# Folding a feature map into two projection weights with 32-row TensorE tiles, in two whole-matrix stretches

## The chip, the cores and the metric

The kernel runs on one core of a Trainium2 chip. The metric is the device time of one execution in microseconds (us), lower is better. A profile's span leaves out about 1.7 us of it. TensorE is called PE, its weight loads PEld, VectorE DVE, ScalarE ACT, GpSimd POOL, SyncE SP. PSUM, where matmuls write, has eight banks of 512 fp32 values in each of 128 partitions (the Trainium skill, "PSUM — Partial Sum Buffer", Specifications; the kernel's pools fit it).

## The reference, cut to what matters

```python
qkv = (x @ wqkv)...                      # x: 2048 x 512, bf16; 32 heads of 16
pq = jnp.einsum('bhsd,hdf->bhsf', q, w_phi)     # a 16x16 map per head
pk = jnp.einsum('bhsd,hdf->bhsf', k, w_phi)
phi_q = concat([softmax(pq), softmax(-pq)])     # phi_k likewise; linear attention follows
...
z = gelu(x @ w_in)                       # second branch: 2048 x 1376
z1, z2 = z[..., :688], layernorm(z[..., 688:])
g = w_sp @ z2 + b_sp                     # mixes along the sequence
return gate * attention(...) @ wo + (1 - gate) * (z1 * g) @ w_out
```

As `q @ w_phi` is `x @ (wq @ w_phi)`, the kernel multiplies `w_phi` into `wq` and `wk` once, on the chip, and then projects `x` with the folded weights. That fold is what changes.

Of the kernel before, what the change touches and what calls it, by code (L numbers as in the profile page):

```python
# [14 lines left out]
P = 128  # L15
# [8 lines left out]
NDT = D // P  # L24
CH = 512
# [10 lines left out]
def kernel(  # L36
# [14 lines left out]
    nc = tc.nc  # L51
# [14 lines left out]
    wq_p = pers.tile([P, NDT, D], BF16, name="wq_p")  # L66
    wk_p = kvw.tile([P, NDT, D], BF16, name="wk_p")
# [3 lines left out]
    wqkT = early.tile([P, 8, D], BF16, name="wqkT")  # L71
    wphiE = early.tile([P, H, DH], BF16, name="wphiE")
    eexp = early.tile([P, P], BF16, name="eexp")
    wphi = early.tile([P, NDT, P], BF16, name="wphi")
# [32 lines left out]
        out=ramp[:, 0, :], data0=ones32[:, :], data1=zeros[:, :], initial=0.0,  # L107
# [4 lines left out]
    for q in range(4):  # L112
        qs = slice(32 * q, 32 * q + 32)
        nc.vector.tensor_tensor(
            out=ident[qs, qs], in0=ramp[qs, 0, :], in1=ramp[qs, 1, :], op=ALU.is_equal)
# [3 lines left out]
    def load_z2w(eng, dt):  # L119
# [10 lines left out]
        out=xs[:, 2:4, :], in_=x2[2 * P:4 * P, :].rearrange("(i p) d -> p i d", p=P))  # L130
    for h in range(2):
        nc.sync.dma_start(
            out=w_z1[:, 2 * h:2 * h + 2, :], in_=w_in_v[:, 2 * h:2 * h + 2, 0:FH])
    for i in range(4, 8):
        nc.sync.dma_start_transpose(out=xT[:, :, i * P:(i + 1) * P], in_=x2[i * P:(i + 1) * P, :])
    for q in range(2, NCH):
        nc.sync.dma_start_transpose(
            out=xT[:, :, q * CH:(q + 1) * CH], in_=x2[q * CH:(q + 1) * CH, :]
# [4 lines left out]
        out=wv_sb[:, :, :],  # L143
        in_=A_wqkv[:, 2 * D:3 * D].rearrange("(dt p) n -> p dt n", p=P),
    )
    for q in range(NCH):
        nc.sync.dma_start_transpose(
            out=wspT[:, :, q * CH:(q + 1) * CH], in_=B_w_sp[q * CH:(q + 1) * CH, :]
# [4 lines left out]
        out=eexp[:, :], in_=eexp[:, :], pattern=[[0, 8], [-1, 16]],  # L153
# [4 lines left out]
        out=mask_bd[:], in_=mask_bd[:], pattern=[[-16, 8], [0, 16]],  # L158
# [3 lines left out]
        out=mask_bd[:], in_=mask_bd[:], pattern=[[16, 8], [0, 16]],  # L162
# [4 lines left out]
        out=mask4[:], in_=mask4[:], pattern=[[-32, NG]],  # L167
# [3 lines left out]
        out=mask4[:], in_=mask4[:], pattern=[[32, NG]],  # L171
# [3 lines left out]
        out=mask64[:, :, :], in_=mask4[:, :, None].to_broadcast([P, NG, DH]))  # L175
# [7 lines left out]
    def next_turn(kind, n):  # L183
        turn[kind] += 1
        return f"{kind}{(turn[kind] - 1) % n}"

    def zp_tile():
        return psA.tile([P, 2, CH], FP32, name="zp", tag=next_turn("zp", 3))

    def pq_tile(shape, dtype=FP32):  # L190
        return psF.tile(shape, dtype, name="pq", tag=next_turn("pq", 2))
# [24 lines left out]
    def z2_tile(tt):  # L216
        z2_out(tt, z_mm(tt, w_z2, FH + 1))

    def z2_first_two():
        zps = [zp_tile() for _ in range(2)]  # L220
        tp1 = psA.tile([P, 2, P], BF16, name="tp1", tag=next_turn("zp", 3))
        turn["zp"] -= 1

        def warm_up(n, w=CH):
            for _ in range(n):
                nc.tensor.matmul(  # L226
                    zps[0][:, 1, 0:w], lhsT=nc.const_aps.tensor(1.0, [P, P], BF16),
                    rhs=nc.const_aps.tensor(1.0, [P, w], BF16), start=True, stop=True)

        def one(tt, dt, j):  # L230
            z_one(zps[tt], tt, w_z2, FH + 1, dt, j)

        warm_up(6)
        warm_up(5, P)
        x_T(0, 0, 1, pq_tile([P, 1, P], BF16)[:, :, :])
        x_T(0, 1, NDT, pq_tile([P, 3, P], BF16)[:, :, :], on_act=True)
        warm_up(3, P)
        one(0, 0, 0)
        x_T(1, 0, 2, tp1[:, :, :])
        x_T(1, 2, NDT, pq_tile([P, 2, P], BF16)[:, :, :], on_act=True)  # L240
        one(0, 1, 0)
        warm_up(2, P)
        one(1, 0, 0)
        one(1, 1, 0)
        gate_T()
        one(0, 2, 0)
        one(1, 2, 0)
        for dt in range(2):
            one(0, dt, 1)
            one(1, dt, 1)  # L250
        one(0, 2, 1)
        one(1, 2, 1)
        x_T(2, 0, NDT, pq_tile([P, NDT, P], BF16)[:, :, :])
        one(0, 3, 0)
        one(0, 3, 1)
        z2_out(0, zps[0])
        one(1, 3, 0)
        one(1, 3, 1)
        z2_out(1, zps[1])
        x_T(3, 0, NDT, pq_tile([P, NDT, P], BF16)[:, :, :])  # L260

    def z1_tile(tt):
        zp = z_mm(tt, w_z1, FH)
        nc.scalar.activation(  # L264
            out=z1all[:, tt, :].rearrange("p (j n) -> p j n", j=2), in_=zp[:, :, 0:HF],
            func=AF.Gelu_apprx_tanh,
        )

    def z2_norm(ts):
        sl = slice(ts[0], ts[-1] + 1)  # L270
        nc.gpsimd.tensor_scalar(
            out=veps[:, sl], in0=mv[:, sl, 1], scalar1=1e-5, scalar2=None, op0=ALU.add
        )
        nc.gpsimd.tensor_tensor(out=rstd[:, sl], in0=veps[:, sl], in1=mhalf[:, sl], op=ALU.pow)
        for tt in ts:
            nc.vector.tensor_scalar(
                out=z2all[:, tt, :], in0=z2all[:, tt, :],
                scalar1=mv[:, tt, 0:1], scalar2=rstd[:, tt:tt + 1],
                op0=ALU.subtract, op1=ALU.mult,
            )  # L280
# [16 lines left out]
    def b_T():  # L297
        bt = pq_tile([P, NT])
        nc.tensor.matmul(bt[:, :], lhsT=brow[:, :], rhs=ident[:, 0:NT], start=True, stop=True)
        nc.vector.tensor_copy(out=bT[:, :], in_=bt[:, :])  # L300

    def wphi_fold():
        wps = pq_tile([P, NDT, P])
        for kc in range(NDT):
            nc.tensor.matmul(  # L305
                wps[:, kc, :], lhsT=eexp[:, :],
                rhs=wphiE[:, kc * 8:(kc + 1) * 8, :].rearrange("e h f -> e (h f)"),
                start=True, stop=True,
            )
        nc.vector.tensor_tensor(  # L310
            out=wphi[:, :, :], in0=wps[:, :, :],
            in1=mask_bd[:, None, :].to_broadcast([P, NDT, P]), op=ALU.mult,
        )

    def fold(qk, dt):
        dst = wq_p if qk == 0 else wk_p
        fps = pq_tile([P, CH])
        for kc in range(NDT):
            nc.tensor.matmul(  # L319
                fps[:, kc * P:(kc + 1) * P],  # L320
                lhsT=wqkT[:, qk * 4 + kc, dt * P:(dt + 1) * P],
                rhs=wphi[:, kc, :],
                start=True, stop=True,
            )
        if dt % 2 == 1:
            nc.scalar.copy(out=dst[:, dt, :], in_=fps[:, :])
        else:
            nc.vector.tensor_copy(out=dst[:, dt, :], in_=fps[:, :])

    with tc.manual_schedule(engines={mybir.EngineType.PE, mybir.EngineType.Activation}):  # L330
        z2_first_two()
        z2_tile(2)
        z2_tile(3)
        b_T()
        for c in range(NCH):
            ts = list(range(c * 4, c * 4 + 4))
            for tt in ts:
                if c > 0:
                    z2_tile(tt)
                if c >= 2 and tt % 2 == 0:  # L340
                    fold(3 - c, (tt % 4) // 2)
            for tt in ts:
                z1_tile(tt)
                if c >= 2 and tt % 2 == 0:
                    fold(3 - c, 2 + (tt % 4) // 2)
            z2_norm(ts)
            if c == 1:
                wphi_fold()
# [264 lines left out]
```

## The kernel before: the parts that the change touches

The first stage makes 32 z tiles (16 for z2, 16 for z1) from 8 matmuls each, in four groups c = 0..3 of four z2 and four z1 tiles. A z tile takes two PSUM banks, and three such buffers (`zp0` to `zp2`) rotate. Two single banks (`pq0`, `pq1`) serve everything else of the stage. That is all eight banks. PE and ACT run in program order. DVE's order is chosen by the scheduler at build time.

```python
def zp_tile():
    return psA.tile([P, 2, CH], FP32, name="zp", tag=next_turn("zp", 3))

def pq_tile(shape, dtype=FP32):
    return psF.tile(shape, dtype, name="pq", tag=next_turn("pq", 2))

def z2_out(tt, zp):                      # gives the buffer zp back
    z2v = z2all[:, tt, :].rearrange("p (j n) -> p j n", j=2)
    nc.scalar.activation(out=z2v, in_=zp[:, :, 0:HF], func=AF.Gelu_apprx_tanh)
    nc.vector.tensor_copy(out=glog[:, tt:tt + 1], in_=zp[:, 1, HF:HF + 1])   # "the glog copy"
    for j in range(2):
        nc.vector.bn_stats(out=bn6[:, tt, j, :], in_=z2v[:, j, :])
    nc.vector.bn_aggr(...)
# z1_tile: 8 matmuls into a zp, then one gelu on ACT gives it back
# z2_norm(ts): POOL makes rstd, then DVE normalises the group's four z2 tiles

def fold(qk, dt):                        # 128 rows of a folded weight
    dst = wq_p if qk == 0 else wk_p
    fps = pq_tile([P, CH])
    for kc in range(NDT):
        nc.tensor.matmul(
            fps[:, kc * P:(kc + 1) * P],
            lhsT=wqkT[:, qk * 4 + kc, dt * P:(dt + 1) * P],
            rhs=wphi[:, kc, :],          # 128x128, eight 16x16 blocks on the diagonal
            start=True, stop=True,
        )
    # copied out by DVE (even dt) or ACT (odd dt)
...
    for c in range(NCH):
        ...
        for tt in ts:
            if c > 0: z2_tile(tt)
            if c >= 2 and tt % 2 == 0: fold(3 - c, (tt % 4) // 2)
        for tt in ts:
            z1_tile(tt)
            if c >= 2 and tt % 2 == 0: fold(3 - c, 2 + (tt % 4) // 2)
        z2_norm(ts)
        if c == 1: wphi_fold()           # 4 matmuls that lay out w_phi, in a pq bank
```

The softmax here doesn't subtract the row's maximum and nothing guards it: scores larger than these inputs give would overflow.

## Time and profile before

| | before |
|---|---|
| median of 3 runs | 208.36 us (208.36 to 209.25) |
| span of the profiled run | 207.5 us |
| PE busy | 203.6 us, 98% |
| a z tile on PE | 1.17 us |
| a fold on PE, of 8 | 0.225 us |

From the page of the kernel before: busy time of each engine with its share of the span, the clock granted to TensorE in 40 slices of the span (9 is 90% or more), and the engines of the chain of waits that ended last.

```profile
PE 203.6 (98%) x1456; PEld 122.5 (59%) x1456; DVE 131.4 (63%) x282; ACT 75.4 (36%) x122; POOL 46.6 (22%) x78
...
PEclk9999999999999999999999999999999999999999
...
PE 98%; DVE 0%; issue 0%
```

PE is the limit from end to end, at full clock.

The timeline of the kernel before around the first two folds. The columns are start, duration, engine, line, operation, what it writes from what, shapes, and count; the brackets give idle time of the engine and what ended it.

```profile
26.61 0.39 PE L319 MATMUL pq<-wphi,wqkT 128*128 128x128 bf16 x4
...
26.84 2.50 PE L195 MATMUL zp<-w_z,xT 128*128 128x344 bf16 x16
27.04 0.69 DVE L328 CAST wk_p<-pq 128x512 bf16<-128x512 f32 x1 [0.61 <-PE pq L319]
...
28.21 0.74 ACT L210 ACTIVATE z2all<-zp 128x688 bf16<-128x688 f32 x1 [0.65 <-PE zp L195]
...
28.98 0.16 DVE L211 COPY glog<-zp 128x1 f32<-128x1 f32 x1
...
29.06 0.93 DVE L213 BATCH_NORM_STATS2 bn<-z2all 128x6 f32<-128x344 bf16 x2
29.18 0.39 PE L319 MATMUL pq<-wphi,wqkT 128*128 128x128 bf16 x4
...
30.02 0.58 ACT L326 CAST wk_p<-pq 128x512 bf16<-128x512 f32 x1
```

Read the starts, as durations of PE reach into the next instruction: 26.61 to 26.84 is one fold, and PE rows show no idle time. The z2 tile that ends at 28.01 (halfway through the 16 matmuls) is given back at 29.14, when its glog copy is done: 1.13 us later. The folds write pq, so none of this touches them.

Near its end the same kernel already uses row tiles, 64 rows high, in its output stage. From the timeline of PE of the kernel before:

```profile
146.74 1.24 PE L496 MATMUL mm<-wspT,uT 128*128 128x512 bf16 x5
147.91 0.61 PE L499 MATMUL mm<-wspT,uT 64*128 64x512 bf16 x4
148.45 1.04 PE L366 MATMUL mm<-wq_p,xT 128*128 128x512 bf16 x4
```

Five 512-column matmuls 0.216 us apart end at 147.82; the 64-row ones start at 147.91, so entering the mode cost 0.09 us. The four of them, two pairs side by side, and the way out take 0.54 us.

### The profile page before, as it was taken

The page shows a single profiled execution, that of the slowest core. Times are in us where ns is not written, and L with a number is a line of the kernel's source. Part 1 is how long each engine was busy: PE and PEld are TensorE (multiplying, and loading weights), DVE is VectorE, ACT ScalarE, POOL GpSimd, SP SyncE. Part 2 cuts the span into 40 slices and gives each one's busy share as a digit, 9 for nine tenths or more (in the row PEclk, how much of TensorE's full clock was granted, in tenths as well). Part 3 has the DMA queues.
Part 4 walks back from the last instruction along what each step waited for, and adds up shares of the span by engine and source line. Part 5 has one row for each costly group of instructions (what it writes and reads, how often), then busy time and mean ns, then how long its engine had stood idle before and what let it go on. Part 6 is the DMA issues. An engine that isn't in the chain of part 4 may idle for free.

```text
span 207.5 us, 3776 instructions
## 1 busy us (share of the span) xinstructions
PE 203.6 (98%) x1456; PEld 122.5 (59%) x1456; DVE 131.4 (63%) x282; ACT 75.4 (36%) x122; POOL 46.6 (22%) x78
## 2 busy tenths in 40 slices
PE   8999999999999999999999999999999999999994
PEld 4666666765566555556565666555455555665642
DVE  2477786764977777879797788555466563633330
ACT  3665666666422232333323033222251126002322
POOL 7020202020542227243342422222204220200000
PEclk9999999999999999999999999999999999999999
DMA  6999999999922014971403236753564469253442
GB/s 189 263 187 202 242 290 218 267 284 179 290 38 43 0 38 89 254 179 33 92 18 71 50 41 115 144 106 70 108 160 89 76 114 182 56 104 65 132 89 77
DMA packets 88970, 27.20 MB, mean 131 GB/s; under 512 B 82968, under 2 KB 88952, under 8 KB 88952
## 3 DMA queue, kind: packets, MB, share of 16 engines
q1 hardware_dynamic: 86176, 24.37, 59.1%
q10 hardware_dynamic: 2744, 2.60, 4.3%
q8 instruction: 11, 0.18, 0.4%
q14 instruction: 7, 0.06, 0.1%
q0 software_dynamic: 32, 0.00, 0.0%
HBM read 4.41 MB, written 2.10 MB: 31 GB/s over the span
## 4 chain that ended last, share of the span: by engine, by line
PE 98%; DVE 0%; issue 0%
PE mm L457 36%; PE zp L195 18%; PE mm L366 13%; PE mm L496 8%; PE mm L494 7%; PE mm L406 7%; PE at L470 2%; PE kvacc L422 2%; PE zp L226 2%; PE mm L499 1%; PE pq L319 1%; PE pq L284 1%; DVE ob L506 0%; PE pq L305 0%; PE tp L284 0%
## 5 line engine op out<-in xcount | busy, mean ns | idle before, releaser
L457 PE MATMUL mm<-z2all,wspT 128*128 128x344 bf16 x512 | 79.9, 309 | 0.0
L457 PEld LDWEIGHTS <-wspT 128*128 128x128 bf16 x512 | 49.0, 98 | 25.7 <-issue 0.4
L195 PE MATMUL zp<-w_z,xT 128*128 128x344 bf16 (+1 forms) x256 | 40.6, 312 | 0.0
L370 ACT ACTIVATE eq<-mm 128x512 bf16<-128x512 f32 x32 | 17.4, 594 | 51.3 <-POOL eq L383 21.5
L374 DVE TENSOR_REDUCE zs<-eq 128x64 f32<-128x1024 bf16 x16 | 19.5, 1220 | 20.3 <-ACT eq L370 20.3
L195 PEld LDWEIGHTS <-xT 128*128 128x128 bf16 x256 | 24.7, 99 | 11.2
L462 DVE SCALAR_TENSOR_TENSOR ucat<-mm,bT,z1all 128x344 bf16<-128x344 f32 x32 | 17.4, 544 | 21.8 <-PE mm L457 21.8
L383 POOL TENSOR_TENSOR eq<-eq,ratio 128x512 bf16<-128x512 bf16 x16 | 16.9, 1058 | 50.2 <-DVE ratio L382 41.7
L370 ACT ACTIVATE ek<-mm 128x512 bf16<-128x512 f32 x32 | 17.3, 600 | 27.1 <-PE mm L366 27.1
L510 ACT ACTIVATE ob<-mm,g_inv 128x512 bf16<-128x512 f32 (+1 forms) x16 | 10.9, 681 | 32.8 <-PE mm L499 28.3
L374 DVE TENSOR_REDUCE zs<-ek 128x64 f32<-128x1024 bf16 x16 | 19.3, 1209 | 2.8 <-ACT ek L370 2.8
L496 PE MATMUL mm<-wspT,uT 128*128 128x512 bf16 (+2 forms) x85 | 20.1, 366 | 0.0
L366 PEld LDWEIGHTS <-xT 128*128 128x128 bf16 x128 | 12.2, 98 | 12.9 <-PE mm L499 0.8
L383 POOL TENSOR_TENSOR ek<-ek,ratio 128x512 bf16<-128x512 bf16 x16 | 16.9, 1059 | 2.0 <-DVE ratio L382 1.2
L494 PE MATMUL mm<-wspT,oT 128*128 128x512 bf16 (+2 forms) x68 | 16.6, 366 | 0.0
L366 PE MATMUL mm<-wq_p,xT 128*128 128x512 bf16 x64 | 16.4, 379 | 0.0
L406 PE MATMUL mm<-wv_sb,xT 128*128 128x512 bf16 x64 | 16.4, 379 | 0.0
L366 PE MATMUL mm<-wk_p,xT 128*128 128x512 bf16 x64 | 16.3, 379 | 0.0
L213 DVE BATCH_NORM_STATS2 bn<-z2all 128x6 f32<-128x344 bf16 x32 | 14.9, 502 | 0.0
L210 ACT ACTIVATE z2all<-zp 128x688 bf16<-128x688 f32 x16 | 11.8, 744 | 7.3 <-PE zp L195 6.8
L264 ACT ACTIVATE z1all<-zp 128x688 bf16<-128x688 f32 x16 | 11.9, 744 | 6.7 <-PE zp L195 6.7
L496 PEld LDWEIGHTS <-uT 128*128 128x128 bf16 x85 | 8.1, 98 | 9.2
(79 smaller groups left out, 150.9 us busy)
## 6 DMA issues: line engine op xcount, KB each, us to landing
out_dram<-ob ACTq DMA_DIRECT2D x15, 128.0 KB, 1.8
wspT<-in_B_w_out_dram SPq DMA_DIRECT2D x2, 640.0 KB, 5.6
w_z<-in_B_w_in_dram SPq DMA_DIRECT2D x2, 344.0 KB, 4.2
w_z<-in_B_w_in_dram ACTq DMA_DIRECT2D x3, 172.0 KB, 3.5
wv_sb<-in_A_wqkv_dram SPq DMA_DIRECT2D x1, 512.0 KB, 4.7
wspT<-in_A_wo_dram SPq DMA_DIRECT2D x1, 512.0 KB, 6.2
xs<-in_A_x_dram SPq DMA_DIRECT2D x2, 128.0 KB, 3.1
xs<-in_A_x_dram SPq DMA_DIRECT2D x1, 256.0 KB, 4.3
```

The costliest lines, as they stand in the source:

```text
L195: nc.tensor.matmul(zp[:, j, 0:n], lhsT=xT[:, dt, tt * P:(tt + 1) * P], rhs=wt[:, dt, j * HF:j * HF + n], start=(dt == 0), stop=(dt == NDT ...
L213: nc.vector.bn_stats(out=bn6[:, tt, j, :], in_=z2v[:, j, :])
L264: nc.scalar.activation(out=z1all[:, tt, :].rearrange("p (j n) -> p j n", j=2), in_=zp[:, :, 0:HF], func=AF.Gelu_apprx_tanh,)
L366: nc.tensor.matmul(ps[:, :], lhsT=xT[:, dt, tt * P:(tt + 1) * P], rhs=w[:, dt, :], start=(dt == 0), stop=(dt == NDT - 1))
L370: nc.scalar.activation(out=e[:, :, a, :], in_=ps[:, :].rearrange("p (h f) -> p h f", f=DH), func=AF.Exp, scale=1.0 - 2.0 * a)
L374: nc.vector.tensor_reduce(out=z[:].rearrange("p h a -> p (h a)"), in_=e[:].rearrange("p h a f -> p (h a) f"), axis=AX.X, op=ALU.add,)
L383: nc.gpsimd.tensor_tensor(out=e[:, :, 1, :], in0=e[:, :, 1, :], in1=ratio[:, :, None].to_broadcast([P, H, DH]), op=ALU.mult)
L406: nc.tensor.matmul(v_ps[:, :], lhsT=xT[:, dt, tt * P:(tt + 1) * P], rhs=wv_sb[:, dt, :], start=(dt == 0), stop=(dt == NDT - 1))
L457: nc.tensor.matmul(gp[:, 0:HF], lhsT=wspT[:, st, tt * P:(tt + 1) * P], rhs=z2all[:, st, j * HF:(j + 1) * HF], start=(st == 0), stop=(st == ...
L462: nc.vector.scalar_tensor_tensor(out=ucat[tt % NU][:, c0 + j * HF:c0 + (j + 1) * HF], in0=gp[:, 0:HF], scalar=bT[:, tt:tt + 1], in1=z1all[ ...
L494: nc.tensor.matmul(acc, lhsT=oT[:, g, :], rhs=wo_t[:, g, c0:c1], start=(g == 0), stop=False)
L496: nc.tensor.matmul(acc, lhsT=uT[:, i + ft, :], rhs=w_main[i][:, ft, c0:c1], start=False, stop=False)
```

## The change

The intent is to waste less of the array: 16x16 blocks in a 128x128 operand are mostly zeros. With 32-row tiles, four matmuls of 32 rows and 32 columns are to work on four row groups at once, and a 128x128 product streams 32 columns instead of 128. Each row group writes its own bank, so a whole folded weight fills four banks: two z buffers. The Trainium skill, "TensorEngine Tiling (Array Packing)", Gotcha 1, says that different row tiles cannot use one PSUM bank at the same time.

```diff
-    def fold(qk, dt):
-        dst = wq_p if qk == 0 else wk_p
-        fps = pq_tile([P, CH])
-        for kc in range(NDT):
-            nc.tensor.matmul(...)          # K=128, N=128
-        if dt % 2 == 1: nc.scalar.copy(out=dst[:, dt, :], in_=fps[:, :])
-        else:           nc.vector.tensor_copy(out=dst[:, dt, :], in_=fps[:, :])
+    def fold(qk):
+        dst = (wq_p if qk == 0 else wk_p)[:].rearrange("p dt n -> p (dt n)").rearrange(
+            "p (m r f) -> p r m f", r=4, f=32)
+        fps = [zp_tile() for _ in range(2)]
+        for m in range(NDT * NDT):
+            dt, kc = divmod(m, NDT)
+            for r in range(4):
+                rows = slice(32 * r, 32 * r + 32)
+                nc.tensor.matmul(
+                    fps[r // 2][:, r % 2, m * 32:(m + 1) * 32],
+                    lhsT=wqkT[rows, qk * 4 + kc, dt * P:(dt + 1) * P],
+                    rhs=wphi[rows, kc, rows], start=True, stop=True,
+                )
+        for h in range(2):
+            src = fps[h][:, :, :].rearrange("p r (m f) -> p r m f", f=32)
+            if h == 0: nc.vector.tensor_copy(out=dst[:, 0:2], in_=src)
+            else:      nc.scalar.copy(out=dst[:, 2:4], in_=src)
...
-                if c >= 2 and tt % 2 == 0: fold(3 - c, (tt % 4) // 2)
+                if c >= 2 and tt % 4 == 1: fold(3 - c)
...
-                if c >= 2 and tt % 2 == 0: fold(3 - c, 2 + (tt % 4) // 2)
```

More of the change, by code (lines that the diff above doesn't have):

```diff
@@ L313, in wphi_fold @@
         )
-    def fold(qk, dt):
-        dst = wq_p if qk == 0 else wk_p
-        fps = pq_tile([P, CH])
-        for kc in range(NDT):
-            nc.tensor.matmul(
-                fps[:, kc * P:(kc + 1) * P],
-                lhsT=wqkT[:, qk * 4 + kc, dt * P:(dt + 1) * P],
-                rhs=wphi[:, kc, :],
-                start=True, stop=True,
-            )
-        if dt % 2 == 1:
-            nc.scalar.copy(out=dst[:, dt, :], in_=fps[:, :])
-        else:
-            nc.vector.tensor_copy(out=dst[:, dt, :], in_=fps[:, :])
+    def fold(qk):
[13 more added lines that the diff above has]
+            src = fps[h][:, :, :].rearrange("p r (m f) -> p r m f", f=32)
+            if h == 0:
+                nc.vector.tensor_copy(out=dst[:, 0:2], in_=src)
+            else:
+                nc.scalar.copy(out=dst[:, 2:4], in_=src)
     with tc.manual_schedule(engines={mybir.EngineType.PE, mybir.EngineType.Activation}):
@@ L339 @@
                     z2_tile(tt)
-                if c >= 2 and tt % 2 == 0:
-                    fold(3 - c, (tt % 4) // 2)
+                if c >= 2 and tt % 4 == 1:
+                    fold(3 - c)
             for tt in ts:
                 z1_tile(tt)
-                if c >= 2 and tt % 2 == 0:
-                    fold(3 - c, 2 + (tt % 4) // 2)
             z2_norm(ts)
```

## The prediction

> **What bounds the kernel now.** TensorE: the page gives PE 203.6 us busy of 207.5 (98%), the chain of waits is 98% PE, the granted clock is 1.0 throughout. What is added to PE's order goes 1:1 into the total. The folds lie between 26.6 and 44.8 us. There the timeline shows PE without a gap: a z tile (8 matmuls of 344) every 1.17 us, a fold (4 matmuls of 128 columns, 56 ns apart) 0.225 us. Eight folds are 1.8 us, 0.9% of the span: all that PE can win.
>
> **What the change does.** 32 matmuls of K=128, N=128 become 128 of K=32, N=32 on four row groups, in two stretches of 64. Eight 512-element copies (DVE 0.68 us, ACT 0.58 us) become four of 1024, by estimate from those times 1.2 us on DVE, 1.1 on ACT. The targets move from the pq banks, which nothing else used then, into two of the three z buffers. Each stretch stands behind the second z2 tile of its group.
>
> **The matmuls.** The 64-row pairs near the end of before show such tiles: the second of a pair starts about 4 ns after the first; switching into the mode and out of it costs about 0.09 us each over the usual spacing of 0.216 us. The Trainium skill, "TensorEngine Tiling (Array Packing)", Key Properties, says that changing the mode drains TensorE; the trace agrees. If four row tiles overlap, 16 rounds of about 32 ns (the spacing of before's 68-column matmuls) are 0.5 us, with the switches 0.7 a stretch, against 0.9 for four folds. Without overlap: 64 x 32 ns, 2.1 us.
>
> **Buffers decide.** z2 tiles n, n+1 take A, B; the fold takes C, A; tile n+2 takes B, n+3 takes C. Counted from the end of tile n+1 on PE:
> - B is free after its gelu on ACT (starts at +0.21, lasts 0.74) and DVE's glog copy: +1.13 in before. Tile n+2 starts at about 1.15 however short the fold; PE idles about 0.45 us.
> - C is free after DVE's 1024-element copy, which stands behind glog and two bn_stats of tile n+1 (end about +1.98) in DVE's order, so ends at about 3.2. PE is ready for tile n+3 at 2.3 and waits about 0.9 us.
> - ACT's copy of A ends at about 2.1, in time.
>
> Tile n+3 starts at 3.25; less one tile, 2.1 us of overhead against 0.9 before: +1.2 us a stretch, +2.4 in all. Overlap of the small matmuls hardly matters: without it, +1.4 to 1.6 each. Nothing later has slack to take it up.
>
> **Prediction: 210.8 us**, 8 times in 10 between 209.5 and 212.2. Faster by over 2%: 0.01; within 2%: 0.93; slower by over 2%: 0.06.
>
> **What would show it right or wrong.**
> - Fold matmuls about 4 to 10 ns apart, a stretch 0.5 to 0.8 us. Near 30 ns: no overlap.
> - Two idle times of PE a stretch: about 0.4 us after the fold (releaser glog copy or gelu), about 0.9 us before the second z2 tile after it (releaser DVE's fold copy). PE idle up by 2.5 to 3 us in all.
> - DVE fold copies of 1.2 us, right behind bn_stats.
> - First exp matmul to the end unchanged within 0.5 us.
>
> **What would make it wrong.** A DVE copy that starts earlier or runs faster (209.5 or less); small matmuls over 30 ns apart or mode switches inside the stretch (212 or more); idle time that lowers the granted clock; the later stage shifted against its transposing DMAs.

## The result, and the profile after

| | before | with the change |
|---|---|---|
| median | 208.36 us (208.31 to 209.25, 4 runs) | 211.04 us (210.87 to 211.20, 4 runs) |
| ratio | 1 | 1.0118 (95% interval 1.0090 to 1.0147) |
| span of the profiled run | 207.5 us | 209.2 us |
| w_phi layout to last z matmul (trace) | 20.56 us | 22.73 us |
| from there to the end (trace) | 161.67 us | 161.66 us |

A ratio is the mean time of one kernel's runs over that of the other's in the same rounds, so it is not quite the ratio of the medians. Executions over 1.5% slower than the fastest of the same kernel are left out of the means.

The last two rows are the ruler. It runs from the start of the first of the four w_phi layout matmuls to the start of the last z matmul, both read from single records of the trace; it is called *the stretch* below. (The first expectations measure to the first exp matmul instead, 0.14 us later; in several traces that record is missing and the next one, 0.216 us on, was read, among them the 23.10 us there.) Such an expectation has to be compared with the stretch plus 0.14 us. The head of the kernel, ahead of the stretch, scatters from run to run, 24.56 to 25.88 us over all fourteen profiles, so the stretch tells small differences apart that the total time cannot. The profiled run of before had a head of 25.22 us, that with the change 24.80; this is why the spans differ by 1.7 us and the stretch by 2.17.

From the page with the change: busy time, and the engines of the chain that ended last.

```profile
PE 201.8 (96%) x1534; PEld 120.8 (58%) x1552; DVE 131.1 (63%) x280; ACT 75.3 (36%) x120; POOL 46.4 (22%) x78
...
PE 91%; DVE 3%; DMA 2%; ACT 1%; issue 1%; SPq 0%
```

DVE and ACT have entered the chain. The 1.8 us by which PE is less busy are not what the fold saves: in the stretch PE is busy for about 20.6 us in both traces. 0.9 us of it lie in the head, and 0.95 us behind the stretch, where the trace with the change lacks 18 matmul records. Who PE waited for (sum in us, times, longest), first before, then with the change:

```profile
PE zp L226 <- PEq L597: 0.8, 1, 0.8
```

```profile
PE zp L195 <- DVE glog L211: 0.9, 2, 0.4
...
PE zp L195 <- DVE wq_p L331: 0.6, 1, 0.6
PE zp L195 <- DVE wk_p L331: 0.6, 1, 0.6
PE zp L195 <- DMA w_z<-in_B_w_in_dram: 0.4, 1, 0.4
```

In the table of before, that one line, at the start of the kernel, is all: no z matmul (L195) appears. The last line with the change is a wait for weights in the head, at 6.2 us, which comes and goes (e_mix has it; e_mix_5, the same kernel, has not) and has nothing to do with the fold. The timeline with the change, around the first fold:

```profile
27.46 0.66 PE L323 MATMUL zp<-wphi,wqkT 32*128 32x32 bf16 x64
27.56 0.74 ACT L210 ACTIVATE z2all<-zp 128x688 bf16<-128x688 f32 x1 [0.43 <-PE zp L195]
...
28.23 1.01 ACT L333 CAST wk_p<-zp 128x1024 bf16<-128x1024 f32 x1
28.34 0.16 DVE L211 COPY glog<-zp 128x1 f32<-128x1 f32 x1
28.41 0.93 DVE L213 BATCH_NORM_STATS2 bn<-z2all 128x6 f32<-128x344 bf16 x2
28.55 1.33 PE L195 MATMUL zp<-w_z,xT 128*128 128x344 bf16 x8 [0.43 <-DVE glog L211]
...
29.26 1.21 DVE L331 CAST wk_p<-zp 128x1024 bf16<-128x1024 f32 x1
...
30.52 1.77 PE L195 MATMUL zp<-w_z,xT 128*128 128x344 bf16 x11 [0.64 <-DVE wk_p L331]
```

The tile ahead of the fold ended on PE at 27.36. The 64 small matmuls are over by 27.94. The next z tile wants the buffer of the tile ahead of the fold, and starts at 28.55, just behind that tile's glog copy. The tile after it wants the fold's first buffer, and starts at 30.52, just behind DVE's fold copy, which stood behind two bn_stats. The chain of waits with the change, in order of time, runs through exactly these (start, length, what):

```profile
28.41 0.08 DVE glog L211
28.50 0.84 DVE bn L213 x2
29.34 1.13 DVE wk_p L331
30.47 0.04 issue
30.52 7.18 PE zp L195 x48
```

The second stretch, from 38.79 us on, repeats the picture to within 0.01 us.

### The profile page after: what moved, and what is told of

Read it like the earlier page. It is cut to its first block, busy times and chain, and to the rows that moved or that the text cites. A ratio compares the mean times of both kernels' runs of the same rounds, so it can differ in the third digit from the quotient of the medians.

```text
span 209.2 us, 3947 instructions
## 1 busy us (share of the span) xinstructions
PE 201.8 (96%) x1534; PEld 120.8 (58%) x1552; DVE 131.1 (63%) x280; ACT 75.3 (36%) x120; POOL 46.4 (22%) x78
## 4 chain that ended last, share of the span: by engine, by line
PE 91%; DVE 3%; DMA 2%; ACT 1%; issue 1%; SPq 0%
PE mm L460 36%; PE zp L195 16%; PE mm L369 13%; PE mm L499 8%; PE mm L409 7%; PE mm L497 7%; DMA w_z<-in_B_w_in_dram 2%; PE at L473 2%; PE kvacc L425 2%; DVE bn L213 2%; PE mm L502 1%; ACT z2all L210 1%; DVE wq_p L331 1%; DVE wk_p L331 1%; DVE glog L211 0%
## 5 line engine op out<-in xcount | busy, mean ns | idle before, releaser
L195 PE MATMUL zp<-w_z,xT 128*128 128x344 bf16 (+1 forms) x256 | 39.2, 309 | 2.6 <-DVE glog L211 0.9
L195 PEld LDWEIGHTS <-xT 128*128 128x128 bf16 x256 | 24.7, 98 | 14.9 <-issue 3.0
L513 ACT ACTIVATE ob<-mm,g_inv 128x512 bf16<-128x512 f32 (+1 forms) x16 | 10.9, 680 | 32.8 <-PE mm L502 28.3
L497 PE MATMUL mm<-wspT,oT 128*128 128x512 bf16 (+2 forms) x62 | 15.6, 365 | 0.3
```

Of the source, the lines that this page charges most:

```text
L195: nc.tensor.matmul(zp[:, j, 0:n], lhsT=xT[:, dt, tt * P:(tt + 1) * P], rhs=wt[:, dt, j * HF:j * HF + n], start=(dt == 0), stop=(dt == NDT ...
L497: nc.tensor.matmul(acc, lhsT=oT[:, g, :], rhs=wo_t[:, g, c0:c1], start=(g == 0), stop=False)
```

## The experiments

The theory is that the loss is waits for z buffers, made by what the fold writes into and by who empties it when. The rival is that the small matmuls and the mode switches themselves are slow. A second rival is the place: two long stretches instead of eight short ones. All kernels gave correct results.

| kernel | matmuls | banks of a fold | stretch, us | PE waits in it, us |
|---|---|---|---|---|
| before | whole | pq, pq | 20.56 | none |
| the change | 32-row | z, z | 22.73 | 0.43 and 0.64, twice |
| e_swap | 32-row | z, z; ACT empties the first | 21.14 | 0.43, twice |
| e_whole_z | whole | z, z | 23.27 | 1.20, twice |
| e_whole_z_swap | whole | z, z; ACT empties the first | 21.14 | 0.13, twice |
| e_whole_mix | whole | pq, pq, z | 20.56 | none |
| e_mix | 32-row | pq, pq, z | 20.16 | none |
| e_pq64 | 64-row, four places | pq, pq | 20.56 | none |

### Which engine empties the buffer that is wanted first (e_swap)

```diff
-            if h == 0: nc.vector.tensor_copy(out=dst[:, 0:2], in_=src)
-            else:      nc.scalar.copy(out=dst[:, 2:4], in_=src)
+            if h == 1: nc.vector.tensor_copy(out=dst[:, 2:4], in_=src)
+            else:      nc.scalar.copy(out=dst[:, 0:2], in_=src)
```

> The measure is the stretch of the trace from the first matmul of the w_phi expansion to the first exp matmul: 20.70 us before, 23.10 us with the change. Buffer theory (the loss is PE waiting for z buffers): if ACT copies the half that lies in the buffer that is wanted first and DVE the other, the second wait of each stretch (0.64 us, released by DVE's fold copy) goes, the first (0.43 us, glog) stays; stretch 21.2 to 21.4 us, time about 0.6 us over before (208.9 to 209.3). Rival (the small matmuls and the mode switches themselves are slow): nothing changes, 23.1 us.

Measured: stretch 21.14 us; 209.32 us against 209.00, ratio 1.0026 (1.0004 to 1.0049). The waits of PE in the stretch, from the table of who waited for whom of this run:

```profile
PE zp L195 <- DVE glog L211: 0.9, 2, 0.4
```

The same matmuls, mode switches and copies, with the engines of two copies exchanged, and 1.6 of the 2.17 us are back. The waits for the fold copy are gone and those for the glog copy have stayed.

### Whole matmuls in the change's place and buffers (e_whole_z)

```diff
-            for r in range(4): ...          # 32-row matmuls
+            nc.tensor.matmul(
+                fps[dt // 2][:, dt % 2, kc * P:(kc + 1) * P],
+                lhsT=wqkT[:, qk * 4 + kc, dt * P:(dt + 1) * P],
+                rhs=wphi[:, kc, :], start=True, stop=True)
...
+        nc.vector.tensor_copy(out=dst[:, 0:2, :], in_=fps[0][:, :, :])
+        nc.scalar.copy(out=dst[:, 2:4, :], in_=fps[1][:, :, :])
```

> The old whole 128x128 matmuls, but in the change's two places and its two z buffers, with the same 1024-element copies. Buffer theory: the loss comes without any 32-row tile; the second wait stays, the first shrinks by what the fold is longer (0.9 against 0.66 us); stretch 23.0 to 23.2 us, time as with the change (210.7 to 211.2). Rival (small matmuls and mode switches): back to before, 20.7 us.

Measured: stretch 23.27 us; 211.55 us against 209.00, ratio 1.0122 (1.0096 to 1.0148). The loss comes whole without a single row tile, which the rival cannot explain. It is larger than expected (about 23.4 us on the ruler of the expectation, against 23.0 to 23.2) and came in another form, one wait of 1.20 us in each stretch. From the table of who waited for whom, and from the timeline of DVE of this run, which tells why:

```profile
PE zp L195 <- DVE glog L211: 2.4, 2, 1.2
```

```profile
28.50 1.17 DVE L325 CAST wk_p<-zp 128x1024 bf16<-128x1024 f32 x1
29.58 0.15 DVE L211 COPY glog<-zp 128x1 f32<-128x1 f32 x1
29.65 0.93 DVE L213 BATCH_NORM_STATS2 bn<-z2all 128x6 f32<-128x344 bf16 x2
```

The scheduler put the fold copy ahead of the glog copy here, so the buffer that waits for glog hung on both.

### The same with the engines exchanged (e_whole_z_swap)

```diff
-        nc.vector.tensor_copy(out=dst[:, 0:2, :], in_=fps[0][:, :, :])
-        nc.scalar.copy(out=dst[:, 2:4, :], in_=fps[1][:, :, :])
+        nc.scalar.copy(out=dst[:, 0:2, :], in_=fps[0][:, :, :])
+        nc.vector.tensor_copy(out=dst[:, 2:4, :], in_=fps[1][:, :, :])
```

> Whole 128x128 matmuls in the two z buffers, with ACT copying the buffer that is wanted first. Buffer theory: the next z tile starts when gelu and glog copy of the tile before the fold are done, 1.15 us after that tile, whether the fold takes 0.68 (32-row) or 0.9 us (whole): stretch to the last z matmul 21.1 to 21.2 us, the same as with 32-row tiles in that form (21.14), idle time after the fold 0.2 to 0.3 instead of 0.43 us. If the length of the fold counted, 21.5 us.

Measured, one look: stretch 21.14 us (209.07 us in all), equal to e_swap to 0.01 us. The whole matmuls take 0.31 us longer than the 32-row ones without the switch out of the mode, and the wait behind them is 0.13 us instead of 0.43 (0.2 to 0.3 was expected); the switch out, 0.10 us, is hidden in the longer wait. While two of three z buffers are held, the fold's own length does not matter, at least between 0.6 and 0.9 us.

### One z buffer instead of two (e_mix), with whole matmuls for comparison (e_whole_mix)

```diff
-        fps = [zp_tile() for _ in range(2)]
+        pqs = [pq_tile([P, CH]) for _ in range(2)]
+        zp = zp_tile()
+        fps = [pqs[0][:, :], pqs[1][:, :], zp[:, 0, :], zp[:, 1, :]]
...
-                    fps[r // 2][:, r % 2, m * 32:(m + 1) * 32],
+                    fps[r][:, m * 32:(m + 1) * 32],
...
+        for r in range(2):
+            nc.vector.tensor_copy(
+                out=dst[:, r], in_=fps[r].rearrange("p (m f) -> p m f", f=32))
+        nc.scalar.copy(out=dst[:, 2:4], in_=zp[...])   # row groups 2 and 3
```

`e_whole_mix` is this with the whole matmuls of `e_whole_z`, a bank for each 128 rows of the weight.

> The change's 32-row matmuls in its places, but row groups 0 and 1 write the two pq banks, which are idle then, and only groups 2 and 3 write a z buffer: one of three taken instead of two. Buffer theory: no wait of PE in the stretch, only the fold's own time of 0.66 to 0.7 us in place of 0.9; stretch 20.2 to 20.4 us, time 0.3 to 0.5 us under before. Rival: the loss stays, about 23 us.

> Whole 128x128 matmuls in the change's two places, with the mixed banks (two pq banks and one z buffer). Buffer theory: 16 matmuls of 56 ns a stretch as before, no waits; stretch 20.7 us, time as before within 0.2 us; the difference to the 32-row version with mixed banks is what the tiling gains, 0.4 us. A theory that the place itself costs (two long stretches instead of eight short ones): over 21.2 us.

Measured: stretches 20.16 and 20.56 us. Times 208.67 and 208.97 us against 209.00, ratios 0.9988 (0.9966 to 1.0010) and 1.0001 (0.9971 to 1.0030). Busy time by engine in a window over both folds of e_mix (window, length, busy us and instructions of PE, then the other engines, the granted clock, DMA):

```profile
26.00:45.00 19.00, 19.00 (x250) 12.75 (x249) 13.47 (x42) 13.08 (x17) 2.53 (x4) 1.00 1.23 251
```

PE is busy all of the time. With no waits in either, the two differ by the matmuls alone: the row tiles gain 0.20 us a stretch, 0.40 in all. And e_whole_mix equals before, so the place costs nothing by itself; that rival falls.

Five rounds were to settle the time of e_mix:

> The same kernel as e_mix (32-row tiles, two pq banks and one z buffer), with five rounds, to tell 0.4 us from nothing: its trace gave a stretch from the w_phi expansion to the last z matmul of 20.16 us against 20.56 before. Expected ratio 0.998, interval below 1 or just touching it.

Measured: stretch 20.16 us again, but 208.99 us against 208.90, ratio 1.0008 (0.9985 to 1.0031; one run of before, 211.77 us, is left out of it): nothing shown. Two likely reasons are in the traces. The head scatters by more than 0.4 us. And after the stretch e_mix takes 161.77 to 161.80 us, not 161.67. It takes 34 z buffers where before takes 32, so the last z1 tile falls into the banks of the second exp matmul group; that group starts 0.13 us late, right after the tile's gelu has ended.

### One buffer skipped, so that the last tiles fall as before (e_mix_shift)

```diff
+            if c == 2:
+                turn["zp"] += 1
```

> e_mix with one z buffer skipped in the rotation before the third group of tiles. In e_mix 34 z buffers are taken instead of 32, so the last z1 tile lies in the banks of the second exp matmul group, which waits 0.13 us for its gelu. With one skipped, the last tiles lie as before. Expected: stretch to the last z matmul still 20.16 us (20.56 before), the rest after it 161.66 us as before instead of 161.78; by the trace 0.4 us under before. Time ratio 0.998; the head of the kernel scatters by more than that, so the interval will probably reach 1.

Measured: stretch 20.16 us, the rest 161.67 us, as expected. 208.39 us (207.85 to 209.07, 6 runs) against 208.88, ratio 0.9974 (0.9947 to 1.0001). Two runs of before in these rounds were slow, 212.02 and 1217.13 us; the ratio leaves them out. In the trace this version beats both kernels, by 0.4 us and 2.6 us. In time its gain over before is at the edge of what six runs show.

### No z buffer at all (e_pq64)

```diff
+        fps = [pq_tile([P, CH]) for _ in range(2)]
+        for m in range(2 * NDT):
+            dt, kc = 2 * half + m // NDT, m % NDT
+            for r in range(2):
+                rows = slice(64 * r, 64 * r + 64)
+                nc.tensor.matmul(fps[r][:, m * 64:(m + 1) * 64], ...)   # four places, not two
```

> No z buffer at all: 64-row tiles, two row groups with 64 columns each, into the two pq banks; that needs four places (half a weight each) and so eight mode switches instead of four. By the trace, 8 rounds of about 30 ns and 0.19 us of switches, 0.43 us a place, 1.7 us against 1.8 before: stretch 20.5 to 20.7 us, within 0.2 us of before, and slower than the 32-row version with mixed banks by about 0.3 us. If the switches were free it would be equal to that.

Measured: stretch 20.56 us, just that of before; 209.27 us against 209.10, ratio 1.0021 (0.9996 to 1.0046). Sixteen 64-row matmuls take 0.22 us from first to last start, half of the two whole folds (0.45 us) that they replace, but the eight switches give the gain back. e_mix, with half as many switches, is 0.40 us shorter.

### The fold behind the z1 tiles (e_z1place, e_z1swap)

```diff
-                if c >= 2 and tt % 4 == 1: fold(3 - c)
             for tt in ts:
                 z1_tile(tt)
+                if c >= 2 and tt % 4 == 1: fold(3 - c)
```

`e_z1swap` is this with the exchange of `e_swap`.

> The change as it is, but each fold stands behind the second z1 tile of its group instead of the second z2 tile. z1 tiles have no glog copy and no bn_stats, so DVE is free for the fold copy at once. Buffer theory: first wait shorter by the glog copy (0.43 to about 0.3 us), second about nothing; stretch 20.8 to 21.1 us, time 0.1 to 0.4 us over before. If the waits came from taking two buffers alone, whatever DVE has queued: as with the change, 23.1 us.

Measured: stretch 24.66 us, 213.25 us against 209.10, ratio 1.0211 (1.0171 to 1.0251). The expectation was wrong by 4 us, because DVE's order for this kernel had not been looked at. The timeline of DVE of this run:

```profile
31.70 0.21 DVE L214 BATCH_NORM_AGGREGATE mv<-bn 128x2 f32<-128x12 f32 x1
33.38 1.57 DVE L276 TENSOR_SCALAR z2all<-z2all,mv,rstd 128x688 bf16<-128x688 bf16 x4 [1.47 <-POOL rstd L274]
34.86 1.22 DVE L331 CAST wk_p<-zp 128x1024 bf16<-128x1024 f32 x1
```

DVE was free from 31.91 us on, but the fold copy, ready at about 32.8, stands behind the normalisation, which waits for POOL. PE waits 1.79 us in each stretch for it.

> The fold behind the second z1 tile, with ACT copying the buffer that is wanted first. In the z1 place DVE's order puts its fold copy behind the normalisation of z2, which waits for POOL; there the buffer wanted second now hangs on it. Expected: no wait for the second tile after the fold; the third waits 0.7 to 0.8 us for DVE's copy in the first stretch; stretch to the last z matmul 21.3 to 21.6 us (24.66 with DVE on the buffer wanted first). If the place itself cost the 4 us, it would stay over 24.

Measured, one look: stretch 21.54 us (209.80 us in all). The waits of PE in this run:

```profile
PE zp L195 <- DVE wk_p L331: 0.6, 1, 0.6
PE zp L195 <- ACT z1all L264: 0.5, 2, 0.2
```

Moving DVE's copy to the buffer that is wanted later takes 3.1 us away; what is left of it is the third tile's wait of 0.63 us, a little under the expected 0.7 to 0.8. This supports the reading of e_z1place: the order on DVE, not the place.

### The price of the small matmuls, and a limit met on the way (e_mix_x3, e_mix_x2)

```diff
-        for m in range(NDT * NDT):
+        for m in [m for _ in range(3) for m in range(NDT * NDT)]:     # e_mix_x2: range(2)
```

> The 32-row version with mixed banks, each fold matmul issued three times over (same result): measures the price of the small matmuls apart from the two mode switches. If 64 of them take 0.5 us as in the trace of the change, the stretch grows by 4 x 0.5 = 2.0 us over the version that issues them once (to about 22.3 us), and the rest of a fold, 0.15 to 0.2 us, is the switches. If they ran 4 at a time at the spacing of 25 ns a group that the start of each fold shows, 1.6 us.

Measured: stretch 36.58 us, 224.99 us against 209.10, ratio 1.0775 (1.0740 to 1.0810). The price itself can be read: the first 169 matmuls of a stretch start within 1.351 us, 8.0 ns apart. Then PE stops, and the profile names no releaser. The waits of PE, and windows before, in and after the first stop (third last number: the granted clock):

```profile
PE pq L325 <- issue: 9.5, 2, 5.2
```

```profile
24.00:30.00 6.00, 6.00 (x204) 4.38 (x201) 3.88 (x12) 3.46 (x5) 0.88 (x1) 1.00 1.29 258
30.00:34.40 4.40, 0.14 (x17) 0.07 (x12) 0.63 (x3) 0.00 (x0) 0.00 (x0) 0.64 1.23 209
34.40:47.00 12.60, 12.60 (x243) 8.23 (x244) 6.77 (x20) 6.96 (x9) 1.26 (x2) 0.85 1.20 244
```

The two stops, 4.3 and 5.2 us, make 9.5 of the 14 us beyond expectation. After each, the z matmuls start 0.287 us apart instead of 0.146 until the clock is granted in full again, at 38.08 and 58.56 us: another 4.5 us. In the trace, packets of 16,384 bytes of the instruction queue land at 33.1 and 50.9 us, and PE goes on at 34.33 and 52.48.

> 32-row version with mixed banks, each fold matmul twice. With three times, TensorE stopped for 4 to 5 us at its 169th matmul of each stretch, released by nothing the profile names; packets of the instruction queue landed 1.2 us before it went on. If TensorE had run out of instructions there, 128 matmuls a stretch should stop shorter or not at all, and the stretch to the last z matmul is 20.16 + 2 x 0.51 = 21.2 us, at 8 ns a matmul. If small matmuls had another limit of time or heat, a stop of over a microsecond would still be there.

Measured, one look: stretch 23.02 us (211.21 us in all). The first stretch of 128 matmuls ran through in 1.009 us; the second stopped once, after 105, for 1.7 us, and went on 1.5 us after an instruction packet had landed at 39.1. So the expectation held for one stretch and not for the other. That PE had run out of instructions fits all three stops and the shorter stop of the shorter stream. The places of the stops fit it too: counted over the whole trace, they come after 351 and 607 matmuls of PE in e_mix_x3 and after 479 in e_mix_x2, so they lie on one grid of 128 matmuls with their 128 weight loads, 256 instructions, wherever that falls in a fold. A limit of time or heat would not explain such a grid. It is still an inference: no record says so, and why the packets came when they did stays open (the DMA share over the two stops of e_mix_x3 reads above 1, so the DMA engines were busy).

## Why the prediction was right

The prediction was right in sign, size and mechanism: +2.4 us predicted, +2.17 in the trace, ratio 1.0118 (about 2.5 us) in the timed runs.

- **PE bounds, and added waits go 1:1 into the total.** Right: the rest of the kernel took 161.67 us before and 161.66 after.
- **The fold itself gets shorter, 0.7 against 0.9 us a stretch.** Right: e_mix against e_whole_mix, 0.20 us a stretch. The switches cost 0.10 us in and about 0.10 out. The matmuls took 0.48 us from first start to last, as expected. Their spacing was near the predicted 4 ns (2 to 5) only inside the first eight groups of four, which start 25 ns apart (the second 39); after that all run evenly 8 ns apart, which comes to nearly the same sum.
- **The first z tile after the fold waits for the glog copy.** Right: start at +1.19 us predicted as 1.15, idle 0.43 as 0.45. e_whole_z_swap shows that the fold's length disappears in this wait.
- **The second waits for DVE's copy, which stands behind two bn_stats.** Right: bn_stats end at +1.98 us as predicted, the tile starts at +3.16 instead of 3.25. e_swap shows the cause by taking the wait away alone. But the place of that copy in DVE's order is the scheduler's choice: in e_whole_z, a near variant, it was another, and e_z1place was missed for that reason. So far as it was assumed, it was luck.
- **Overlap of the small matmuls hardly matters.** Not tested: no run has small matmuls without overlap. That a fold longer by 0.31 us changes nothing is shown, by e_whole_z_swap against e_swap (21.14 us both), while DVE does not hold the buffer that is wanted second. A fold of 2.1 us, the prediction's case without overlap, lies outside what was tried.
- **Total idle up by 2.5 to 3 us.** Slightly off: 0.43 + 0.64 twice is 2.1 us. (The pages differ by 3.5 us of idle time, but 0.4 of it is the DMA wait in the head and 0.95 the missing records.) The copy's end was estimated at 3.2 and was 3.1, and the second idle time was called 0.9 us where the profile counts 0.64, since it counts from the modelled end of a matmul, not from the moment when PE could have started the next.
- **ACT's copy in time.** Right: it ended at 29.24, and its buffer was not wanted before the z tile that follows 30.52.

The median grew by 2.7 us, more than the stretch. The rest most likely lies in the head, since all else agrees in the two traces kept: three of the four runs of before were near 208.3, while before took 208.9 to 209.1 in the median of the later rounds. So the closeness of 211.04 to the predicted 210.8 us is in part luck; the stretch, +2.17 for +2.4, is the fair measure.

## What to carry to other kernels

A faster matmul is worth what its output buffers allow. Before moving work into buffers that rotate, write down for each of the next tiles which buffer it takes, who empties it, and what stands ahead of that in the emptying engine's order; here two idle banks and an exchange of engines were worth more than the tiling. When a scheduler orders an engine, look at the order of every variant, since moving a call can move its copy behind something that waits.

## What the Trainium skill lacked or had wrong

- "TensorEngine Tiling (Array Packing)", Key Properties, says that changing the tiling mode drains TensorE, without a figure. Here the first 32-row matmul starts 0.097 us later than the usual spacing allows, and the first whole matmul after the last 32-row one starts 0.112 us after it, 8 ns of which are its own slot. Eight such switches used up the whole gain of e_pq64.
- The same page, PSUM Bottleneck, advises using both ScalarE and VectorE to empty PSUM. The trace agrees, but that alone was not enough: with both in use, which of them emptied the buffer wanted first made 1.6 us (22.73 against 21.14).
- "TensorE: Matmul & The Clock Gate", Part 3, gives about 4 ns between matmuls of different row tiles. Here that holds inside the first eight groups of four only (2 to 5 ns); a stream of 64 or more settles at 8 ns for each matmul with its weight load, 33 ns a group of four, against 56 ns for the whole 128-column matmul that it replaces.
- "Runtime: NRT & Kernel Launch", Instruction fetch mechanics, says that instructions are refilled in 16 KiB blocks of 256 and that the cost is mostly hidden. The packets of 16,384 bytes are in every trace. With 128 and 192 of these small matmuls in a row, stops of 1.7, 4.3 and 5.2 us ended 1.2 to 1.6 us after such a packet and lay whole multiples of 256 instructions apart; if the inference above is right, it is not hidden for dense small matmuls.
- No page that I found says that an order chosen by a scheduler may differ between near variants of a kernel: the fold copy stood behind bn_stats, ahead of glog, or behind the normalisation, for stretches of 22.73, 23.27 and 24.66 us.
